# A chain of attention and feed-forward on one core: unit 0's first heads in two pieces, w_phi by two queues, unit 1's loads held, and a new order table

## The chip, the core and the metric

The kernel runs on one core of one Trainium2 chip. A core has five engines with an instruction stream each: TensorE (PE, matrix products and transposes; its weight loads are shown apart as PEld), VectorE (DVE), ScalarE (ACT), GpSimd (POOL) and SyncE (SP, which only issues DMAs). DMAs are issued from the queues of SP, ACT and POOL and move data between HBM and the on-chip memory. Engines wait for one another through semaphores; on one engine, instructions run in the order in which they were written.

The metric is the device time of one execution in microseconds (us). Beside it there is a profile of one execution, whose span runs from the first to the last instruction.

## The reference: what is computed

```python
def phi(x):                                            # x: [8, 8, 576, 64], w_phi: [64, 128]
    proj = einsum('bhsd,df->bhsf', x, w_phi)
    proj = proj - max(abs(proj), axis=-1, keepdims=True)
    return concatenate([exp(proj), exp(-proj)], axis=-1)
q_p, k_p = phi(q), phi(k)
kv  = einsum('bhsf,bhsd->bhfd', k_p, v)
z   = sum(k_p, axis=2)
num = einsum('bhsf,bhfd->bhsd', q_p, kv)
den = einsum('bhsf,bhf->bhs', q_p, z)[..., None] + 1e-06
x   = (num / den).transpose(0, 2, 1, 3).reshape(4608, 512)
h   = maximum(maximum(x @ w1, x @ w2), x @ w3)         # w1..w3: [512, 768]
out = h @ w_out                                        # w_out: [768, 512], out: [4608, 512]
```

Eight batches of eight heads go through a linear attention with a feature map of exponentials; the 4608 rows of 512 that come out go through a feed-forward layer whose activation is the greatest of three products.

## The kernel before, in words

**Units.** The 64 heads are worked off in 16 units of four heads (`attention(u)`, lines 435 to 694). A unit's heads are two pairs; a pair's 576 rows by 64 columns lie in nine tiles of 128 partitions (64 columns of each of two heads), so a unit has 18 tiles each of q, k and v. Tiles 0 to 3, 4 to 7, 9 to 12, 13 to 16 and the two tiles 8 and 17 are the groups (`GROUPS`) in which the projections are made.

**A unit's steps.** Load q, k and v. Bring q and k to bf16 (`C`, lines 450 and 475, or a load that casts, line 457). Transpose tiles on PE (`T`, lines 489 and 492) in the batches `BATCHES` of eight, eight and two tiles and copy them out of PSUM (`Tc`, line 495); from unit 4 on a DMA transposes (line 507). Project on `w2` (`G`, lines 529 and 534), take the greatest absolute values on DVE (line 553), and the exponentials of k on ACT (`Ek`, line 547). Form the exponentials of q on ACT (`Eq`, line 626) from a second product (`M`, lines 613 to 618, which uses `wphi_m` or `w2`). Weigh v by the factors `em` on POOL (`vab`, line 588). Then the products k'v (`kvps`, line 642), q'(kv) (`psn`, line 660) and the division on DVE (lines 666 and 667). The result is transposed into `xT`.

**The feed-forward layer.** Nine chunks of 512 rows: two times six `ups` products (line 713) and the products that form the output (`ops`, lines 741 and 746). It works with differences of weights: w2 - w1 and w3 - w1 are formed once (line 784), and the part that w1 contributes to the output is carried by a product w1 w_out made at the front (lines 796 and 810). The chunks are woven between later units.

**Loads at the front.** w_phi goes to two halves of the partitions by two DMAs of ACT's queue (line 359); `phi_weights` (lines 402 to 405) casts both halves into `w2` and the first once more into `wphi_m`. Unit 0's q and k come by SP in halves, a pair of heads each (line 446): q, k, k, q. Unit 1's to 3's q and k are loaded by POOL's queue, which casts on the way (line 457). The four weights of the feed-forward layer also come by POOL's queue (line 418).

**Who sets the order.** The order is written out in the table `PLAN` (lines 94 to 242): a number of a step, a letter for its engine, the buffers or PSUM banks that it takes, and the time at which a planner placed it. `plan` (line 248) reads it; the steps are then written in order of these times, so that the table fixes the order on each engine. Waits come from the data, not from the table. The planner itself isn't part of the file; the costs and delays given to each step are what it worked with. `fill` (line 266) puts fillers into PE's planned gaps while it is early: products of a constant tile that nobody reads (`idler`, line 841).

## Time and profile before

| | |
|---|---|
| three runs | 286.4, 287.06 and 288.28 us, median 287.06 |
| the profiled execution | 289.06 us, its span 287.3 us |
| mean granted TensorE clock | 0.992 |
| PE, PEld, DVE, ACT, POOL busy | 276.2, 157.3, 209.5, 192.4, 133.1 us |
| read from HBM, written to it | 34.67 MB, 9.44 MB |

How to read it: an engine's busy time is the time covered by its instructions, issues and waits not counted. A matmul's shown duration overlaps the next one's, so PE's busy share is an upper bound of its work. "idle before, releaser" says what ended an engine's idle time. A wait put down to "issue" is one for which the profile shows nothing that was waited for.

### The profile page before, as it was taken

How to read it: one execution, taken by the hardware profiler on the slowest of the kernel's cores; microseconds unless marked ns; L12 is line 12 of the kernel's file. 1: busy time of each engine (PE TensorE's matmuls, PEld its weight loads, DVE VectorE, ACT ScalarE, POOL GpSimd, SP SyncE). 2: the span in 40 equal slices, each digit the busy share in tenths (PEclk: the TensorE clock that was granted, in tenths of full speed). 3: DMA queues.
4: the chain of work that ended last, by engine and by line, in shares of the span. 5: the costliest groups of instructions: out<-in, count | busy, mean ns of one | idle time of the engine just before them, and what ended most of it. 6: DMA issues, size and time to landing. Idle time of an engine off the chain costs nothing.

```text
span 287.3 us, 8483 instructions
## 1 busy us (share of the span) xinstructions
PE 276.2 (96%) x3501; PEld 157.3 (55%) x3540; DVE 209.5 (73%) x441; ACT 192.4 (67%) x449; POOL 133.1 (46%) x119
## 2 busy tenths in 40 slices
PE   8989999999999799999999999999999999999994
PEld 3667675556665455556555555556544654444443
DVE  2899899988999677998599779968873462355330
ACT  3899899988889668877968969859469300130001
POOL 9359999769676045739171964600235001000000
PEclk9999999999999889999999999999999999999999
DMA  7999999999799999999998688474361014621334
GB/s 200 200 284 268 276 231 281 302 306 264 260 274 216 232 135 251 208 240 232 275 258 213 152 142 158 87 115 90 68 171 39 3 39 91 146 51 24 67 99 127
DMA packets 63728, 50.81 MB, mean 177 GB/s; under 512 B 46154, under 2 KB 50378, under 8 KB 63690
## 3 DMA queue, kind: packets, MB, share of 16 engines
q1 hardware_dynamic: 56686, 35.51, 56.0%
q0 software_dynamic: 6160, 13.76, 18.8%
q10 hardware_dynamic: 844, 1.00, 1.0%
q8 instruction: 27, 0.44, 0.6%
q14 instruction: 11, 0.09, 0.1%
HBM read 34.67 MB, written 9.44 MB: 154 GB/s over the span
## 4 chain that ended last, share of the span: by engine, by line
PE 89%; ACT 4%; DVE 3%; DMA 2%; issue 1%
PE ups L713 32%; PE ops L746 16%; PE ops L741 10%; PE psn L660 7%; PE kvps L642 6%; PE psm L613 5%; PE psq L534 5%; PE idler L841 3%; DMA qkT<-mT 2%; PE pm L810 2%; ACT Ek L547 2%; ACT Eq L626 2%; PE psq L529 1%; DVE mk L553 1%; DVE mqp L553 1%
## 5 line engine op out<-in xcount | busy, mean ns | idle before, releaser
L713 PE MATMUL ups<-xT,w_bf 128*128 128x512 bf16 x412 | 101.4, 379 | 1.0
L588 POOL TENSOR_TENSOR vab<-v_raw,em 128x1152 bf16<-128x1152 f32 (+1 forms) x36 | 68.0, 1904 | 47.8 <-ACT em L584 27.3
L626 ACT ACTIVATE Eq<-psm 128x512 bf16<-128x512 f32 (+1 forms) x160 | 81.0, 596 | 8.9 <-PE psm L613 8.6
L547 ACT ACTIVATE Ek<-psk 128x512 bf16<-128x512 f32 x128 | 73.5, 624 | 7.5 <-DVE mk L553 3.5
L713 PEld LDWEIGHTS <-w_bf 128*128 128x128 bf16 x432 | 40.3, 98 | 42.8 <-DVE x_sb L667 0.3
L746 PE MATMUL ops<-wout_bf,hT 128*128 128x512 bf16 (+1 forms) x214 | 51.9, 381 | 0.5 <-issue 0.2
L553 DVE TENSOR_REDUCE mqp<-psq 128x4 bf16<-128x512 f32 (+1 forms) x80 | 49.2, 632 | 4.2 <-PE psq L529 2.1
L719 DVE TENSOR_TENSOR hT<-hT,ups 128x512 bf16<-128x512 bf16 x54 | 36.2, 683 | 14.8 <-PE ups L713 13.3
L553 DVE TENSOR_REDUCE mk<-psk 128x4 f32<-128x512 f32 x64 | 42.9, 683 | 2.9 <-ACT Ek L547 2.0
L754 ACT COPY osb<-ops 128x512 f32<-128x512 f32 (+1 forms) x19 | 10.9, 575 | 39.5 <-PE ops L746 36.1
L746 PEld LDWEIGHTS <-hT 128*128 128x128 bf16 x222 | 21.6, 99 | 23.9 <-issue 1.6
L667 DVE TENSOR_TENSOR x_sb<-psn,rden 128x320 bf16<-128x320 f32 x64 | 31.5, 492 | 2.2
L660 PEld LDWEIGHTS <-Eq 128*128 128x128 bf16 x640 | 26.2, 98 | 11.5 <-issue 2.5
L660 PE MATMUL psn<-kv_sb,Eq 128*128 128x65 bf16 x640 | 28.3, 194 | 2.0 <-ACT Ek L547 2.0
L721 ACT ACTIVATE hT<-ups 128x512 bf16<-128x512 f32 x26 | 15.9, 622 | 19.9 <-PE ups L713 19.9
L723 DVE TENSOR_SCALAR hT<-ups 128x512 bf16<-128x512 f32 x28 | 18.9, 686 | 11.9 <-PE ups L713 11.7
L754 DVE COPY osb<-ops 128x512 f32<-128x512 f32 (+1 forms) x18 | 12.0, 674 | 20.0 <-PE ops L746 17.4
L741 PE MATMUL ops<-xT 128*128 128x512 bf16 x88 | 24.4, 384 | 0.4
L613 PE MATMUL psm<-qkT,wphi_m 128*128 128x512 bf16 (+1 forms) x70 | 22.4, 360 | 0.1
L534 PE MATMUL psq<-w,qkT 64*128 64x128 bf16 x256 | 21.4, 218 | 0.2 <-DVE qkT L495 0.2
L534 PE MATMUL psk<-w,qkT 64*128 64x128 bf16 x256 | 21.0, 217 | 0.5 <-DVE mqp L553 0.4
L642 PE MATMUL kvps<-vab,Ek 64*128 64x65 bf16 x1152 | 20.4, 190 | 0.6 <-issue 0.4
(76 smaller groups left out, 276.6 us busy)
## 6 DMA issues: line engine op xcount, KB each, us to landing
out_dram<-osb SPq DMA_DIRECT2D x65, 128.0 KB, 2.4
v_raw<-in_v_dram SPq DMA_DIRECT2D x13, 576.0 KB, 5.9
k_raw<-in_k_dram POOLq DMA_DIRECT2D x6, 576.0 KB, 5.6
q_raw<-in_q_dram POOLq DMA_DIRECT2D x6, 576.0 KB, 5.6
q_raw<-in_q_dram SPq DMA_DIRECT2D x6, 576.0 KB, 5.7
k_raw<-in_k_dram SPq DMA_DIRECT2D x6, 576.0 KB, 5.2
w_bf<-in_moe_w_dram POOLq DMA_DIRECT2D x3, 768.0 KB, 11.1
v_raw<-in_v_dram POOLq DMA_DIRECT2D x3, 576.0 KB, 12.2
```

Of the source, the lines that this page charges most:

```text
L534: nc.tensor.matmul(ps()[:, i, :], lhsT=cols[r, :], rhs=w2[r, c, :], start=True, stop=True)
L547: nc.scalar.activation(Ek[s]()[:, tiles_of(t0, n), :], of(1), EXP, scale=1.0 - 2.0 * s)
L553: nc.vector.tensor_reduce((mq, mk)[c]()[:, tiles_of(t0, n)], of(c), AXX, ALU.max, apply_absolute_value=True)
L588: (nc.vector if n_.eng == "DVE" else nc.gpsimd).tensor_tensor(vab()[:, g, t0:t1, 0:D], vb()[:, t0:t1, :], em()[:, g, t0:t1].unsqueeze(2).t ...
L613: nc.tensor.matmul(psm()[:, 0:w], lhsT=wphi_m, rhs=rhs, start=True, stop=True)
L626: nc.scalar.activation(Eqb()[s][:, cols], psm()[:, 0:w], EXP, scale=1.0 - 2.0 * s)
L642: nc.tensor.matmul(kvps[ab]()[:, t // NT, g, :], lhsT=Ek[g]()[r, t, :], rhs=vab()[r, g, t, :], start=(t + g == 0), stop=(t == UT - 1 and g ...
L660: nc.tensor.matmul(psn()[:, c, :], lhsT=Eqb()[g][:, t0:t0 + P], rhs=kv()[:, pr, ab, g, :], start=(g == 0), stop=(g == 1))
L713: nc.tensor.matmul(ups(), lhsT=w_bf[i + 1][:, ct, j * P:(j + 1) * P], rhs=tokens_of(ct), start=(ct == 0), stop=(ct == CT - 1))
L719: nc.vector.tensor_tensor(hT()[:, j, :], hT()[:, j, :], ups(), ALU.max)
L741: nc.tensor.matmul(ops_()[:, 0:width], lhsT=tile_of(ct, tt), rhs=line_w[c_i > MOVE][:, ct, cols], start=(ct == 0), stop=False)
L746: nc.tensor.matmul(ops_()[:, 0:width], lhsT=hT()[:, j, tt * P:(tt + 1) * P], rhs=wout_bf[:, j, cols], start=False, stop=(j == JT - 1))
```

## The change

- Unit 0's q and k come in three pieces each instead of two halves: tiles 0 to 3 and 4 to 8 of the first pair, and the second pair whole. Each piece has its own load on SP's queue and its own cast; the order on SP is q's first piece, k's first piece, q's second pair, k's second piece, q's second piece, k's second pair, then v of unit 0, which POOL's queue carried before.
- Unit 0's transposes go in batches of four, four, eight and two tiles instead of eight, eight and two; a projection waits for the batch of its own group.
- The second half of w_phi is loaded from POOL's queue, as its first DMA. The cast into `wphi_m` is a step of its own.
- The first load of unit 1 on POOL's queue, and so every load behind it, waits for a one-partition copy on DVE that reads k's first piece and writes into the buffer that the load fills.
- The casting loads of units 0 to 3 lose their split in halves (only unit 0 used it). Evictions of transposes may also go to ACT.
- The first fillers may be half as wide, and the last 0.3 instead of 0.2 of planned time ahead of the first transposes stay free.
- `PLAN` is a new table. Against the old one, w_out and w2 leave POOL's queue much later, w2 and w3 as two issues in a row; loads of v, q and k change places between SP's and POOL's queues; some evictions and copies change engine. In the last 3943 of PE's 7082 instructions the order is the same.

```diff
+BATCHES0 = [(0, 4), (4, 4), (9, 8), (8, 2)]
+PIECES = [(0, 0, 4), (0, 4, 9), (1, 0, 9)]
...
-HALVES = 1
+HELD = 0
...
-SLOW = 4.6
+SLOW = 6.0
...
+        wide = 4
         gap, t = n.start - free, max(free + 0.1, ready)
-        while gap > (0.35 if t < WARM else 0.5) and t < n.start - 0.2:
+        while gap > (0.35 if t < WARM else 0.5) and t < n.start - (0.2 if free else 0.3):
...
-                    todo.append((t, make(i)))
+                    wide = 4 if free or t < n.start - 0.9 else 2
+                    todo.append((t, make(i, wide)))
...
-            t += 0.26 if t > SLOW else 0.43
+            t += 0.26 if t > SLOW else 0.11 * wide
...
+    def piece_of(what, p, c0, c1):
+        return (q, k)[what][0, 2 * p:2 * p + 2].rearrange("ab (i c) d -> (ab i) c d", c=NT)[:, c0:c1, :]
...
-    for ab in range(2):
-        nc.scalar.dma_start(wphi_f[ab * D:(ab + 1) * D, :], w_phi)
+    nc.scalar.dma_start(wphi_f[0:D, :], w_phi)
+    nc.gpsimd.dma_start(wphi_f[D:P, :], w_phi)
...
-        nc.vector.tensor_copy(wphi_m[0:D, :], wphi_f[0:D, :])
+    def phi_rows(n_):
+        copy_on[n_.eng](wphi_m[0:D, :], wphi_f[0:D, :])
...
+            if what < 2 and u == 0:
+                for i, (p, c0, c1) in enumerate(PIECES):
+                    ts = slice(NT * p + c0, NT * p + c1)
+
+                    def main(what=what, ts=ts, p=p, c0=c0, c1=c1, raw=raw):
+                        queue_of["SP"].dma_start(raw()[:, ts, :], piece_of(what, p, c0, c1))
...
+                    first[what, i] = n_
...
+            elif what < 2 and by_pe:
+                if u == 1 and what == 0:
+                    src = raw_bufs(0)[1]
+                    need = [nd("gate", {"DVE": 0.1}, lambda src=src: nc.vector.tensor_copy(
+                        qk()[0:1, :, 0, 0:1], src()[0:1, 0:2, 0:1]), [first[1, HELD]], [src, qk])]
+                elif u > 1:
+                    need = []
+
+                def main(what=what):
+                    nc.gpsimd.dma_start(by_pairs(qk()[:, what, :, :]), rows_of(what, u, 0, 2))
...
-            for i, (t0, nb) in enumerate(BATCHES):
+            batches = BATCHES if u else BATCHES0
+            for i, (t0, nb) in enumerate(batches):
...
-                need = [0, 1] if nb == 2 else [i]
+                need = ([1, 2] if nb == 2 else [i]) if u == 0 else [0]
...
-            a = nd("G", {"PE": 0.22 if n == 2 else 0.236 * len(part)}, lambda mms=mms: [f() for f in mms], [tr[ti], n_phi],
+            a = nd("G", {"PE": 0.22 if n == 2 else 0.236 * len(part)}, lambda mms=mms: [f() for f in mms], [tr[ti] if u else tr[part[0]], n_phi],
```

## The prediction

> **What bounds the kernel now.** I read the page first (busy shares, 40 slices), then a table of stretches, then the instructions in order of time for the first 14 us and for the one stretch that stands out.

> ```profile
> PE 276.2 (96%) x3501; PEld 157.3 (55%) x3540; DVE 209.5 (73%) x441; ACT 192.4 (67%) x449; POOL 133.1 (46%) x119
> PE   8989999999999799999999999999999999999994
> PEclk9999999999999889999999999999999999999999
> ```

> TensorE (PE) is busy for 96% of the span, so a change pays only where PE isn't doing useful work: at the front, and in the one slice with a 7 (the fourteenth, from 93 us), behind which the granted clock has two 8s. The stretches say what stands beside PE at each stage. Columns: stretch, length, busy time (and instructions) of PE, PE's weight loads, DVE, ACT, POOL, granted clock, DMA share, GB/s.

> ```profile
> 0.00:8.00 8.00, 6.96 (x26) 2.81 (x27) 2.45 (x14) 3.30 (x4) 7.30 (x15) 1.00 0.78 196
> 8.00:16.00 8.00, 7.64 (x124) 5.03 (x122) 7.13 (x16) 6.92 (x15) 2.22 (x4) 1.00 1.18 211
> 16.00:24.00 8.00, 6.89 (x145) 5.17 (x144) 8.00 (x17) 7.86 (x25) 5.79 (x7) 1.00 1.15 272
> 24.00:32.00 8.00, 7.51 (x200) 5.25 (x193) 7.13 (x18) 7.04 (x19) 7.96 (x9) 1.00 1.13 283
> 32.00:40.00 8.00, 7.89 (x156) 5.98 (x159) 7.36 (x19) 7.26 (x18) 8.00 (x6) 1.00 1.12 266
> 40.00:60.00 20.00, 19.68 (x292) 11.06 (x293) 18.29 (x36) 19.47 (x47) 17.87 (x12) 1.00 1.05 269
> 60.00:94.00 34.00, 33.54 (x499) 20.46 (x505) 30.89 (x69) 29.78 (x72) 24.26 (x21) 1.00 1.04 267
> 94.00:102.00 8.00, 5.99 (x106) 3.30 (x100) 4.00 (x9) 4.24 (x11) 0.00 (x0) 0.79 1.29 210
> ```

> So: loads until 8; DVE and ACT (8.00 and 7.86 of 8 us) at 16 to 24; PE from 24 to 94, where its idle time is 0.49 + 0.11 + 0.32 + 0.46 = 1.38 us; a loss of 2 us and of clock at 94 to 102.

> The front, in order of time (start, duration, engine, line, operation; q behind an engine is its queue's issue):

> ```profile
> 0.72 1.25 ACTq L359 DMA_DIRECT2D wphi_f<-in_w_phi_dram  x2
> 0.72 0.40 SPq L446 DMA_DIRECT2D q_raw<-in_q_dram  x1
> 1.04 5.83 PE L841 MATMUL idler<-idle 128*128 128x512 bf16 x14 [1.04 <-DVE idle L411]
> 1.18 0.89 SPq L446 DMA_DIRECT2D k_raw<-in_k_dram  x2
> 1.89 0.93 POOL L457 DMA_DIRECT2D qk_bf<-in_k_dram  x1
> 2.12 0.61 SPq L446 DMA_DIRECT2D q_raw<-in_q_dram  x1
> 2.81 0.74 POOL L457 DMA_DIRECT2D qk_bf<-in_q_dram  x1
> 3.43 0.67 ACT L450 CAST qk_bf<-q_raw 128x576 bf16<-128x576 f32 x1
> 3.75 0.22 DVE L404 CAST w<-wphi_f 64x128 bf16<-64x128 f32 x1 [1.76 <-DMA wphi_f<-in_w_phi_dram]
> 5.00 0.67 ACT L450 CAST qk_bf<-k_raw 128x576 bf16<-128x576 f32 x1 [0.90 <-DMA k_raw<-in_k_dram]
> 5.83 0.22 DVE L404 CAST w<-wphi_f 64x128 bf16<-64x128 f32 x1 [1.86 <-DMA wphi_f<-in_w_phi_dram]
> 6.81 0.61 PE L489 MATMUL tps<-ident,qk_bf 128*128 128x128 bf16 x8
> 7.45 0.69 DVE L495 COPY qkT<-tps 128x1024 bf16<-128x1024 bf16 x1 [0.95 <-PE tps L489]
> 8.43 0.23 PE L534 MATMUL psq<-w,qkT 64*128 64x128 bf16 x1
> 8.68 0.67 ACT L450 CAST qk_bf<-q_raw 128x576 bf16<-128x576 f32 x1 [1.02 <-DMA q_raw<-in_q_dram]
> 8.86 1.29 DVE L553 TENSOR_REDUCE mqp<-psq 128x4 bf16<-128x512 f32 x2 [0.71 <-PE psq L534]
> 9.26 2.05 ACT L547 ACTIVATE Ek<-psk 128x512 bf16<-128x512 f32 x4
> 10.06 0.28 DVE L495 COPY qkT<-tps 128x256 bf16<-128x256 bf16 x1
> 11.14 0.73 POOL L471 DMA_DIRECT2D q_raw<-in_q_dram  x1 [0.72 <-DMA qk_bf<-in_q_dram]
> 11.84 1.24 PE L492 MATMUL tps<-ident,qk_bf 128*64 128x128 bf16 x32
> ```

> The reader is to see a chain: k's half lands at 5.00, is cast, is transposed at 6.81 (PE still worked off fillers until 6.87), evicted by 8.14, and the first projection starts at 8.43. Unit 1's transposes follow at 11.84, once its q has landed shortly before 11.14.

> **The change part by part.** In the built programs PE has 7082 rows before and after, and from row 3139 (a psm of unit 8, about 105 us) on they are the same; DVE and ACT agree from the same time on, POOL and SP some 10 and 20 us later. No PE operation goes; 26 fillers stay 26, three at half width. So what is gained must be gained ahead of 105 us, and the rest is shifted.

> *First heads in pieces.* k's first piece is SP's second issue, at 1.18. It has 4/9 of the half's bytes. The half of q took 0.72 to 3.43, 2.7 us; that of k 1.18 to 5.00, 3.8; and w_phi, 32 KB, 3.0. Smallness alone buys little, then: 2.7 to 3.8, and I take 2.7, the row of a half that had the queue to itself, since two small pieces now stand first: it lands at 3.9 (5.0). Cast of 256 columns of 576: 0.67 x 4/9 = 0.30, to 4.2. Four transposes, half of 0.61: 4.5. Eviction of 512 columns lies between 0.28 and 0.69: 0.42, so 4.9, and two hand-overs like that before 8.43 (0.29) add 0.6: first projection at 5.6, upper end 6.8. The fillers ahead of it fall from 14 to nine, three of them halves: (6 + 1.5) x 5.83 / 14 = 3.1 us, over at 4.2, out of the way.

> *Half of w_phi by GpSimd's queue.* Both halves now leave ACT's queue 0.6 us apart, yet the second is usable at 5.83, 2.1 us after the first. Issued first on POOL it should come like the first half, at 3.75; at worst it stays at 5.83, and since the eviction stands behind its cast on DVE, the projection would start at 5.83 + 0.22 + 0.42 + 0.3 = 6.8. I take 3.75, the nearest row of a first transfer on its queue. [...] No row here decides it, since both halves went through one queue.

> *DVE and ACT.* DVE's first reduction moves from 8.86 by the same 2.8 us. Ahead of unit 1 it gets two casts (0.30 + 0.37), a one-element copy (about 0.13) and two half evictions for a whole one (0.84 - 0.69), and gives the 0.28 eviction to ACT: +0.67. Its lead is about 2.1. ACT has four casts in front of its first exponential, the last of the sixth piece on SP, issued near 3.0. It lands at 3.0 + 3.8 = 6.8, if POOL's loads are really out of the way, or at 3.0 + 6.5 = 9.5, if it trails like the last half now (2.12 to 8.68). I take the first: exponentials from 7.5 instead of 9.26, a lead of 1.7; the other end is -0.9.

> *Unit 1's loads held.* POOL's first load waits for a DVE copy that stands behind the first eviction and a cast: about 6.0 instead of 1.89, the second 6.9. Queued behind them on POOL are every other load of that queue: w1, unit 2's q and k, w_out.

> ```profile
> k_raw<-in_k_dram POOLq DMA_DIRECT2D x6, 576.0 KB, 5.6
> w_bf<-in_moe_w_dram POOLq DMA_DIRECT2D x3, 768.0 KB, 11.1
> 29.79 6.29 POOL L784 TENSOR_TENSOR w_bf<-w_bf 128x1024 bf16<-128x1024 bf16 x3
> 40.72 1.46 PE L713 MATMUL ups<-xT,w_bf 128*128 128x512 bf16 x5
> 28.97 0.80 POOL L418 DMA_DIRECT2D w_bf<-in_moe_w_dram  x1
> ```

> A load of 576 KB on POOL takes 5.6 us in the run of the kernel, the held ones took up to 11.1 - 2.8 = 8.3 in the crowd. I take 5.6, the crowd being what is removed: unit 1 complete at 12.5 instead of 11.1, its transposes 0.7 later than 11.84; the other end is 15.2, 3.4 later. DVE has unit 0's reductions (nine more of 0.65) to fill until then, and PE's order puts two psm groups of unit 0 ahead of them. v of unit 0 goes to SP and stops being late.

> *What is handed on.* At 16 to 24 DVE and ACT are full, so the smaller lead, ACT's 1.7, is what they carry; unit 1 gives back 0.7. From 24 to 94 PE has 1.38 us of idle time to win or lose in, and I let the lead through. **Sum: 1.7 - 0.7 = 1.0 us**, ends 1.7 and -0.7.

> *Late fetches.* w2 and w3 now leave as two issues in a row near 29 us, the last w leaving at 28.97 today; five differences of 2.1 (6.29 / 3) follow in one run on POOL. I cost this at nothing: the first `ups` is at 40.72, and the differences are needed one by one. If that cover goes, see the third rival.

> **Against the profiled execution.** It took 289.06 us with a span of 287.3: 1.76 lies around the span and stays. 289.06 - 1.0 = 288.06. That execution lies 2.0 above the median of 287.06; I take the same 1.0 off the median: **286.1**.

> **The hole at 95 us.** It is the largest loss, and I leave it in.

> ```profile
> 95.25 0.50 PE L613 MATMUL psm<-qkT,wphi_m 128*128 128x256 bf16 x2
> 97.70 0.47 PE L660 MATMUL psn<-kv_sb,Eq 128*128 128x65 bf16 x10 [1.95 <-ACT Ek L547]
> 97.70 0.35 PEld L660 LDWEIGHTS <-Eq 128*128 128x128 bf16 x9 [2.24 <-issue]
> 98.50:102.00 3.50, 3.50 (x13) 0.51 1.36 270
> ```

> PE stands 1.95 us inside ten matmuls, and then has half the clock for 3.5 us: 1.95 + 0.49 x 3.5 = 3.7 us. The view names an ACT result, yet PE's weight loads stand for 2.24 us with nothing to wait for ("issue"), so I read it as a hold-up in getting instructions to PE, not as work that came late. In the changed order the same `psn` group stands at the same place, row 3010 of 7082, behind the same burst of 72 `kvps`. So I expect it again.

> **The rivals.**
> 1. *The gain is eaten* (0.18). The small pieces land at 5.0, or the last one trails to 9.5, or w_phi comes late, while unit 1 is 0.7 later all the same. For it: 32 KB took 3.0 us. Against it: POOL's loads are out of the way. Time 287.06 + 0 to 0.7: 287.4.
> 2. *The hole goes* (0.15). What comes before it in the queues differs (one load of unit 9 from SP where two stood), so the hold-up may not meet PE's burst. In full: 286.1 - 3.7 = 282.4 (0.08). Half: PE stands still, but the clock stays: 286.1 - 1.7 = 284.4 (0.07). [...]
> 3. *Slower: the late weights hold the MLP* (0.12). The first of the two last w loads, issued at 29 and taking the 11.1 us of its row, lands at 40.1. Its first difference ends 2.1 later, at 42.2, and PE waits 1.5 us at the first `ups`, with a clock dip of 1.7 like the one above: 287.06 - 1.0 + 1.5 + 1.7 = 289.3. It decides from a landing later than 40.72 - 2.1 = 38.6. For it: that load has no slack by the medians. Against it: two of the three w loads in that median stood in the crowd of the front.

> **How the numbers follow.** Forecast 0.55 (286.1, own range 285.4 to 287.8), rivals 0.18, 0.15, 0.12. The range 284.3 to 289.3 leaves out the hole gone in full (0.08) and what lies beyond rival 3 (some 0.08). About 1% is what a measurement of this kernel can tell from no change: 284.2 to 289.9. Faster than that 0.11 (the hole gone, and a little of the forecast), slower 0.07 (half of rival 3), within 0.82.

> **What would show it.** Right: first projection near 5.6, first exponential near 7.5, unit 1's transposes near 12.5, the first `ups` about 1 us before 40.72, the same psm of unit 8 about 1 us earlier, a gap of about 2 us in `psn` near 95. Wrong: casts of the first pieces not before 5; DVE idle behind w_phi; PE idle before unit 1's transposes; `ups` waiting for `w_bf`; slice fourteen without its 7. The forecast fails most easily by the hole: it is nearly four times the sum.

## The result, and the profile after

The changed kernel took 295.27 us (median of four, 293.37 to 295.85), the kernel before beside it 287.56: the ratio is 1.026 with an interval from 1.020 to 1.032, slower by 7.7 us. I had forecast 286.1 with a range up to 289.3. On a second chip it took 294.88 beside 287.52. Medians here are taken over all executions of a kernel, ratios over those that lie within 1.5% of its fastest, so the two can differ. The profiled execution took 295.11 us with a span of 293.3, 6.0 more than the span before.

The page: busy time, PE in 40 slices of 7.3 us, and the granted clock.

```profile
PE 277.7 (95%) x3540; PEld 157.1 (54%) x3540; DVE 212.5 (72%) x446; ACT 191.5 (65%) x445; POOL 136.0 (46%) x125
PE   8777999999999699999699999999999999999994
PEclk9999899999999999999999999999999999999999
```

Where the kernel before had a single 7, there are now three of them at 7 to 29 us, and a 6 at 95 and at 139 us. The stretches (columns as in the prediction):

```profile
0.00:8.00 8.00, 6.29 (x39) 2.65 (x39) 4.42 (x20) 2.72 (x4) 3.00 (x10) 1.00 0.71 213
8.00:16.00 8.00, 6.15 (x99) 3.97 (x100) 6.07 (x13) 7.32 (x19) 2.52 (x5) 1.00 1.11 187
16.00:24.00 8.00, 6.67 (x113) 4.84 (x115) 8.00 (x15) 7.37 (x18) 7.97 (x10) 1.00 1.00 187
24.00:32.00 8.00, 6.35 (x145) 4.75 (x142) 4.93 (x12) 5.42 (x16) 6.95 (x10) 0.79 1.14 273
94.00:102.00 8.00, 5.64 (x127) 3.65 (x126) 5.32 (x13) 5.54 (x11) 4.86 (x4) 1.00 1.19 222
120.00:200.00 80.00, 77.57 (x1086) 44.30 (x1082) 64.90 (x137) 61.55 (x148) 42.14 (x34) 1.00 0.89 195
```

PE does 6.15 us of work at 8 to 16 where it did 7.64, and 6.35 at 24 to 32 where it did 7.51, and the half clock that stood at 98 us now stands in this last stretch (0.79). At 94 to 102 it again lacks more than 2 us, now at full clock. From 120 to 200 it stands still for 2.43 us, where it had 0.68.

The front in order of time:

```profile
4.30 0.23 DVE L414 CAST w<-wphi_f 64x128 bf16<-64x128 f32 x1 [0.89 <-DMA wphi_f<-in_w_phi_dram]
5.26 0.23 PE L558 MATMUL psq<-w,qkT 64*128 64x128 bf16 x1
6.42 0.74 POOL L479 DMA_DIRECT2D qk_bf<-in_q_dram  x1 [3.88 <-DVE qk_bf L473]
8.53 0.67 ACT L465 CAST qk_bf<-k_raw 128x576 bf16<-128x576 f32 x1 [1.54 <-DMA k_raw<-in_k_dram]
9.10 2.05 ACT L571 ACTIVATE Ek<-psk 128x512 bf16<-128x512 f32 x4
13.62 1.20 PE L514 MATMUL tps<-ident,qk_bf 128*64 128x128 bf16 x36
19.50 0.87 POOL L432 DMA_DIRECT2D wout_bf<-in_moe_w_out_dram  x1
```

The first projection starts at 5.26 instead of 8.43. But the first exponential comes at 9.10, only 0.16 sooner than before, and unit 1's transposes at 13.62, 1.8 later. What PE waited for, in the whole span (us in total, times, longest), and the instructions at which it stood still:

```profile
PE psm L637 <- DMA qkT<-mT: 4.8, 2, 2.4
PE tps L511 <- ACT qk_bf L465: 1.7, 2, 1.5
PE psk L558 <- issue: 1.6, 1, 1.6
PE psk L558 <- DVE mqp L577: 1.1, 1, 1.1
```

```profile
28.23 0.11 PEld L558 LDWEIGHTS <-qkT 64*128 64x128 bf16 x3 [1.82 <-issue]
98.65 0.39 PE L637 MATMUL psm<-qkT,wphi_m 128*128 128x512 bf16 x1 [2.36 <-DMA qkT<-mT]
141.79 0.48 PE L637 MATMUL psm<-qkT,wphi_m 128*128 128x256 bf16 x2 [2.43 <-DMA qkT<-mT]
```

Three stops, then, beside the smaller waits of the front: one inside unit 2's first projection at 26.4, in which PE waits for nothing that the profile shows ("issue"), and two for `qkT<-mT`, the small DMA that writes a unit's row of maxima beside its transposed q.

To see how the loss adds up I take the same step in both kernels and subtract the time at which its own table planned it. This lag of PE, in us (from the traces and the tables; the new table ends 0.8 us earlier than the old one):

```
                          before   changed   difference
unit 0's kvps              -0.7      2.8        3.5
first ups                   0.6      6.0        5.4
unit 4's kvps               1.1      6.7        5.6
unit 6's third psm          1.1      9.2        8.1
unit 9's first psm          4.8     12.0        7.1
last product                4.9     11.7        6.8
```

6.8 - 0.8 = 6.0, the difference of the spans. So 3.5 are lost by 25 us (1.75 in time, 25.07 against 23.32; the rest is that the new table planned this step 1.7 earlier); 1.9 more up to the first `ups`, where the changed kernel loses 3.2 with the stop at 26 and its half clock, the kernel before 1.3; 2.5 at 96. The kernel before then loses 3.7 in its own hole, the changed one 2.7 at 139.

### The profile page after: what moved, and what is told of

Read it like the earlier page. It is cut to its first block, busy times and chain, and to the rows that moved or that the text cites. A ratio compares the mean times of both kernels' runs of the same rounds, so it can differ in the third digit from the quotient of the medians.

```text
span 293.3 us, 8525 instructions
## 1 busy us (share of the span) xinstructions
PE 277.7 (95%) x3540; PEld 157.1 (54%) x3540; DVE 212.5 (72%) x446; ACT 191.5 (65%) x445; POOL 136.0 (46%) x125
## 4 chain that ended last, share of the span: by engine, by line
PE 80%; DMA 7%; ACT 4%; SPq 4%; DVE 3%; issue 1%; DVEq 0%
PE ups L737 31%; PE ops L770 14%; PE ops L765 9%; PE kvps L666 6%; PE psn L684 6%; DMA qkT<-mT 5%; PE psm L637 5%; PE psq L558 4%; SPq L531 2%; ACT Ek L571 2%; DMA k_raw<-in_k_dram 2%; PE pm L834 2%; DVE mqp L577 1%; PE psq L553 1%; DVE mk L577 1%
## 5 line engine op out<-in xcount | busy, mean ns | idle before, releaser
L737 PE MATMUL ups<-xT,w_bf 128*128 128x512 bf16 x432 | 102.6, 379 | 0.0
L747 DVE TENSOR_SCALAR hT<-ups 128x512 bf16<-128x512 f32 x30 | 20.4, 685 | 11.9 <-PE ups L737 11.7
L684 PE MATMUL psn<-kv_sb,Eq 128*128 128x65 bf16 x640 | 28.9, 195 | 0.0
L745 ACT ACTIVATE hT<-ups 128x512 bf16<-128x512 f32 x24 | 14.4, 617 | 19.2 <-PE ups L737 19.0
L558 PEld LDWEIGHTS <-qkT 64*128 64x128 bf16 x512 | 14.8, 94 | 14.7 <-issue 10.8
## 6 DMA issues: line engine op xcount, KB each, us to landing
v_raw<-in_v_dram SPq DMA_DIRECT2D x8, 576.0 KB
v_raw<-in_v_dram POOLq DMA_DIRECT2D x8, 576.0 KB, 5.9
q_raw<-in_q_dram SPq DMA_DIRECT2D x8, 576.0 KB, 4.3
k_raw<-in_k_dram SPq DMA_DIRECT2D x7, 576.0 KB
k_raw<-in_k_dram POOLq DMA_DIRECT2D x5, 576.0 KB, 6.6
w_bf<-in_moe_w_dram POOLq DMA_DIRECT2D x3, 768.0 KB, 9.7
q_raw<-in_q_dram POOLq DMA_DIRECT2D x4, 576.0 KB, 6.9
```

The lines of the kernel that those rows point to most:

```text
L558: nc.tensor.matmul(ps()[:, i, :], lhsT=cols[r, :], rhs=w2[r, c, :], start=True, stop=True)
L684: nc.tensor.matmul(psn()[:, c, :], lhsT=Eqb()[g][:, t0:t0 + P], rhs=kv()[:, pr, ab, g, :], start=(g == 0), stop=(g == 1))
L737: nc.tensor.matmul(ups(), lhsT=w_bf[i + 1][:, ct, j * P:(j + 1) * P], rhs=tokens_of(ct), start=(ct == 0), stop=(ct == CT - 1))
```

## The experiments

### The changed kernel once more

> The changed kernel unaltered, on the same chip and beside the same runs of the kernel before as the three kernels below, since its runs so far and those of the first experiments lay on different chips. Theory: 295 within 1 us, the mean granted clock 0.988 to 0.994 in nearly all executions (one or two windows of 3.4 us at half clock each), the stop inside unit 2's first projection near 26 us in the profile again. Rival (bad luck in the first four executions): 291 to 293 and a clock of 1.0 in half of them.

Measured: 294.88 us (four executions, 290.54 to 296.87), ratio 1.017 (1.008 to 1.027), clocks 0.988 to 0.994 in all four. The stop is at the same instruction, 2.3 us. It was not bad luck in the sense of the rival, though one of the four took 290.54. Here no half clock followed it; it followed the wait at 94 us instead.

### The stop in the front: 84 rows more on PE

A row is one instruction of PE's program, a weight load or a matmul (a few only wait). The first 16 fillers are cut into products of a quarter of the width:

```diff
     def product(i, wide):
+        made.append(i)
+        cuts = wide if len(made) <= 16 else 1
...
+            for c in range(cuts):
-            nc.tensor.matmul(idler[:, 0:wide * P], lhsT=idle, rhs=idle.unsqueeze(1).to_broadcast([P, wide, P]),
+                nc.tensor.matmul(idler[:, c * w * P:(c + 1) * w * P], lhsT=idle,
+                                 rhs=idle.unsqueeze(1).to_broadcast([P, w, P]), start=True, stop=True)
```

> The changed kernel, with its first 16 fillers written as several products of a quarter of the width: the same PE time, 42 matmuls with their weight loads more, so that everything behind them stands 84 rows later in PE's program. Theory (instruction transfers): the changed kernel's stop of 1.8 us inside unit 2's first projection at 26.4 us, and the 3.4 us of half clock behind it, come from a block of 256 PE instructions that was asked for only at 25.85, in the middle of the 72 kvps, and arrived too late; moved by 84 rows, the border of the block lies ahead of the kvps burst, the stop goes, and with it the half clock: 3.0 to 3.5 us less, near 291.8. A new stop may then appear where another border falls right behind a kvps burst (near 180 us). Rival (late data): the projection waits for a PSUM bank or for DVE; then the stop stays at the same instruction and the time within 1 us of 295.3.

Measured: 290.28 us (median of eight, 288.27 to 295.06), ratio to the kernel before 1.010 (1.007 to 1.014): 5.0 less than the changed kernel (4.7 less, if each is taken against the kernel before beside it). The profiled execution was the longest of the eight (it lost some 4 us at 68 us to a row of maxima and a half clock behind it), so only its front is read here, PE in order of time and two of its waits:

```profile
25.32 1.27 PE L666 MATMUL kvps<-vab,Ek 64*128 64x65 bf16 x72
26.43 0.22 PE L558 MATMUL psq<-w,qkT 64*128 64x128 bf16 x1
26.85 0.28 PE L639 MATMUL psm<-qkT,w 128*128 128x256 bf16 x1
```

```profile
PE pm L834 <- DMA wout_bf<-in_moe_w_out_dram: 1.3, 1, 1.3
PE tps L514 <- DMA qk_bf<-in_k_dram: 1.0, 1, 1.0
```

The eight products of the projection run through and `psm` follows 0.42 us after the first of them: the stop is gone, without a change to any data or wait. In seven of the eight executions the granted clock was 0.997 or more. Part of the gain is taken back at once: at 28.3 PE waits for w_out, a wait that the stop had hidden. No stop came near 180 us. The gain is larger than the 3.0 to 3.5 that the stop and its half clock account for. In this one profile, SP's order being as it was, the waits for the rows of maxima of units 6 and 9 are smaller too, 0.89 us at 101 and none for unit 9, against 2.36 and 2.43; whether that is the rest of the gain isn't shown.

### The same in the kernel before

The first 14 fillers in quarters, also 84 rows.

> The kernel before, with its first 14 fillers written as four products of a quarter of the width each: again 84 rows more ahead of everything else, and the same PE time. Theory (instruction transfers): the stop of 2 us in psn at 95.6 us and the half clock behind it go, 3.0 to 3.8 us less than the kernel before, near 284. Rival (loads and transposes at 88 to 97 us hold something that PE waits for): the stop stays, and the time stays within 0.5 us of 287.5.

Measured: 286.19 us (median of ten), ratio 0.997 (0.994 to 0.999). The profiled execution has no stop at 95 us and a clock of 1.0; its longest wait behind the front is

```profile
PE psm L613 <- DMA qkT<-mT: 0.9, 1, 0.9
```

The stop went as expected, the gain was a third of what I expected. In 42 of 44 other executions of the kernel before the mean clock was 0.997 or more: the 3.5 us of half clock in its profiled execution (0.992) are not what it usually pays.

### 114 rows: a border where I want it

> The kernel before with 19 of its 26 fillers in quarters: 114 rows more on PE instead of 84. The two borders seen lay at rows 706 and 3010, that is 194 behind a multiple of 256. Shifted by 114 rows, the border at row 2754 falls on the first instructions of unit 6's projection right behind unit 4's kvps, where the kernel before and the shift of 84 have none. Theory (instruction transfers): a stop of 1 to 2.5 us appears there, near 83 us, with a request for instructions inside that kvps burst, and perhaps a shorter one inside unit 6's kvps near 94; 0.5 to 3 us slower than the shift of 84 rows (286.2). Rival (the stops belong to what is done at 26 us and at 95 us, not to rows): no stop at 83 us, and the time within 0.5 us of 286.2.

Measured: 286.07 us (median of ten), ratio 0.996 (0.994 to 0.999), and no stop at the place named:

```profile
82.69 1.26 PE L642 MATMUL kvps<-vab,Ek 64*128 64x65 bf16 x72
83.78 0.22 PE L534 MATMUL psq<-w,qkT 64*128 64x128 bf16 x1
```

So a border behind a burst isn't enough. The DMA records of the trace tell the difference: the request for this block was sent at 77.72, 6 us ahead of the projection.

### 24 rows: does the stop follow the row?

The first four fillers in quarters.

> The changed kernel with only its first 4 fillers in quarters: 12 weight loads and matmuls more, 24 rows. In all six kernels with the rows of the changed kernel PE stood still right behind its 350th weight load, at 25 to 30 us, whatever the front had done before. Theory (instruction transfers, border at a row): the stop stays behind the 350th weight load, which is now one of the last four pairs of unit 0's kvps and no longer the sixth pair of unit 2's projection; 1 to 2.5 us long, the time within 1.5 us of 295. Rival (the projection waits for something): the stop stays in front of the same psk, which is now behind the 362nd weight load. Third: no stop, if the request comes earlier because the border lies inside the burst.

Measured: 294.7 us (292.29 to 297.6). PE in order of time:

```profile
24.11 1.17 PE L666 MATMUL kvps<-vab,Ek 64*128 64x65 bf16 x65
27.32 0.29 PE L666 MATMUL kvps<-vab,Ek 64*128 64x65 bf16 x7 [2.04 <-issue]
```

The stop moved out of the projection into the kvps in front of it, and stands again behind the 350th weight load. The rival is dead: nothing that the projection waits for can stop the kvps. The records of PE's instruction transfers (16 KB each) in ten of the fourteen profiles, against its 350th weight load, behind which this border lies:

```
                    request   350th load   next load   request to next
changed               25.85        26.31       28.23        2.38
changed, again        25.36        25.20       27.79        2.43
SP order              25.29        25.46       27.57        2.28
v on POOL's queue     25.46        26.98       28.09        2.63
not held              30.35        30.22       32.69        2.34
w_phi by ACT          25.87        26.32       28.25        2.38
24 rows               25.07        25.07       27.32        2.25
before                23.56        25.64       25.64
84 rows, changed      22.69        25.82       25.82
84 rows, before       21.22        25.24       25.25
```

Where the request goes out less than 2 us ahead of the 350th load, PE stands still until 2.25 to 2.63 us after the request, though the transfer itself takes 0.9 to 1.1. Where it goes out 2.1 us ahead or more, there is no stop. The border at 95 us in the kernel before lies nine blocks of 256 rows behind this one: its request went out at 94.33, 1.0 us ahead, the transfer took 2.04, and PE went on at 97.70, 3.4 us behind the request.

The same can be counted at every border of all fourteen profiles, 371 of them, with the rows of the built programs. At eleven the request went out less than 2 us ahead, and at each of these the weight loads stood still, for 0.4 to 2.5 us: the seven above, the one at 95 us, and three more between 31 and 41 us that cost 0.4 to 0.5. At the 360 others, with 2.08 us or more, the longest pauses were 0.24, 0.26 and 0.42 us, the last two with the request 8 to 9 us ahead. That a block has 256 rows the traces show by count: in the kernel before the requests at 23.56 and 94.33, for the borders behind rows 706 and 3010, lie nine transfers and 2304 rows apart; its profile and the one after have 27 transfers each for PE's 7082 rows. Why one request leaves 6 us ahead and another in the last moment isn't shown. Waiting for data ahead of the border does not tell them apart: in the 6 us ahead of the stop PE idled for 0.3 us at most in the seven profiles that have it here, in the kernel before, which has none here, for 1.1. What differs is that the burst of 72 `kvps` began 1.2 us ahead of this border in the changed kernel (25.07 and 26.31), 2.3 us ahead in the kernel before (23.32 and 25.64); but with 114 rows a border behind such a burst cost nothing.

### The order on SP

Two places in the table: x of unit 5 (438) behind unit 6's row of maxima (472, at 85.5), and two loads behind unit 9's row (667, at 124.4).

```diff
-438S@84.1 ... 1025S0@121.6 765S1@122.0
+438S@85.6 ... 1025S0@124.5 765S1@124.6
```

SP's queue of the changed kernel, then of the kernel before, at the first place:

```profile
82.38 0.81 SPq L593 DMA_DIRECT2D qkT<-mT  x1
90.86 1.36 SPq L714 DMA_TRANSPOSE xT<-x_sb  x1
92.32 0.78 SPq L593 DMA_DIRECT2D qkT<-mT  x1
93.44 3.40 SPq L531 DMA_TRANSPOSE qkT<-qk_bf  x1
```

```profile
82.03 1.73 SPq L690 DMA_TRANSPOSE xT<-x_sb  x1
86.73 0.80 SPq L569 DMA_DIRECT2D qkT<-mT  x1
```

Before, a transpose of x was issued 4.7 us ahead of the row of maxima, now 1.5 us ahead.

> The changed kernel with another order on SP at two places: the transpose of unit 5's x is issued behind unit 6's row of maxima (qkT<-mT) instead of 1.5 us ahead of it, and the two loads of q and k ahead of unit 9's row of maxima go behind it. Theory (queue order): unit 6's row then lands some 3 us earlier than 98.6 and the wait of psm of 2.4 us at 96 goes; unit 9's row is issued 1.9 us earlier, and the wait of 2.4 us at 139 shrinks to 0.5 or less: 4 to 4.9 us less than the changed kernel, near 290.8. Rival (crowd): unit 6's row is slow because the five POOL loads issued from 81 to 88 us fill the DMA engines until 94; then the first wait stays at 2 us or more and only the second shrinks, near 293.2.

Measured: 291.54 us (four executions, 288.75 to 293.05), ratio 1.014 (1.007 to 1.020), 3.7 less than the changed kernel (3.4 less, each against the kernel before beside it). PE's longest waits:

```profile
PE psk L558 <- issue: 1.8, 1, 1.8
PE psm L637 <- DMA qkT<-mT: 1.3, 1, 1.3
PE ups L737 <- DMA xT<-x_sb: 1.1, 1, 1.1
PE kvps L666 <- POOL vab L612: 0.9, 1, 0.9
```

Both waits for the row of maxima at 96 and 139 us are gone, the first by the exchange of two issues, with POOL's five loads as they were: the crowd is not the reason. They are gone in all three profiles with this order, and at least one of them is there in all eight with the old one, from 0.9 to 4.8 us in total, so the order on the queue is what makes PE wait at these places, and how long it waits depends on more than that. The 1.3 us that are left stand at 106 us, for the row of unit 8, which is issued 1.7 us behind a transpose of x, as unit 6's was. At the second place something else is late now: unit 9's kvps wait for POOL, and a chunk's `ups` for a transpose of x that stands further back on SP.

### Both together

> The changed kernel with both the fillers in quarters (84 more rows ahead on PE) and the new order on SP at two places. If the two causes are independent their gains add: 295.3 - 5.0 - 3.7 = 286.6, level with the kernel before within 0.5 us. If the stop in the front hides behind it waits that the SP order removes too (rival: same loss counted twice), it stays at 289.5 to 290.5. What is left above the kernel before is then the front: PE's lag at unit 0's kvps and at the first pm (waiting for w_out, landed 29.3).

Measured: 292.76 us (290.61, 290.72, 294.8 and 296.45), ratio 1.019 (1.009 to 1.029). The gains don't add: its two best lie where the shift of rows alone lay. The profiled execution (290.72) has neither the stop nor a wait for the row of maxima worth naming. Its waits:

```profile
PE ups L737 <- DMA xT<-x_sb: 1.4, 1, 1.4
PE kvps L666 <- POOL vab L612: 1.3, 1, 1.3
PE pm L834 <- DVE x_sb L691: 1.1, 1, 1.1
```

The last line names DVE, but the product starts at 28.18 and w_out landed at 28.13, so I put this wait down to w_out. POOL, in front of unit 9's kvps:

```profile
130.28 1.14 POOL L496 CAST qk_bf<-q_raw 128x1152 bf16<-128x1152 f32 x1 [6.85 <-DMA q_raw<-in_q_dram]
131.90 4.19 POOL L612 TENSOR_TENSOR vab<-v_raw,em 128x1152 bf16<-128x1152 f32 x2
```

POOL stands 6.85 us at the cast of a q that has not landed, with the products for unit 9 queued behind it. In the changed kernel this was there too (6.59 us), under the wait for the row. This execution's lag is 1.8 at unit 0's kvps, 3.2 at the first `ups`, 4.2 at unit 9's first psm and 7.2 at the end; the 84-row kernel before has 0.1, 0.8, 2.2 and 2.8. 7.2 - 0.8 - 2.8 = 3.6, the difference of their profiled times (290.72 and 286.91) but 0.2. Why two of the four executions took 294.8 and 296.45 isn't shown; neither was profiled.

### The front: unit 1's loads not held

```diff
-                    need = [nd("gate", {"DVE": 0.1}, lambda src=src: nc.vector.tensor_copy(
-                        qk()[0:1, :, 0, 0:1], src()[0:1, 0:2, 0:1]), [first[1, HELD]], [src, qk])]
+                    need = [nd("gate", {"DVE": 0.1}, lambda: None, [first[1, HELD]], [src, qk])]
```

> The changed kernel without the copy on DVE that holds unit 1's first load; POOL's queue starts with w_phi and goes on at once. Theory (the hold costs): unit 1's loads send their first packets near 5.4 us instead of 7.5, all loads behind them (w1, unit 2, w_out, unit 3, w2, w3) land 1.5 to 2 us earlier, w_out near 27.5; PE's lag at unit 0's kvps falls by 0.5 to 1.5 us and the time by 0.5 to 2. Rival (the hold pays): without it k's second pair lands 1 us later than 8.5, the first exponential at 10 instead of 9.1, and the time rises by 0.5 to 1.5.

Measured: 296.64 us (295.3 to 299.55), ratio 1.034 (1.027 to 1.041).

```profile
10.46 0.67 ACT L465 CAST qk_bf<-k_raw 128x576 bf16<-128x576 f32 x1 [3.09 <-DMA k_raw<-in_k_dram]
11.04 1.08 ACT L570 ACTIVATE Ek<-psk 128x512 bf16<-128x512 f32 x2
18.15 1.20 PE L513 MATMUL tps<-ident,qk_bf 128*64 128x128 bf16 x36
```

The rival has it: without the hold the last piece comes 1.9 us later, and unit 1's q and k land at 10.9 and 13.6, little different from with it (11.4 and 13.0). Unit 1's transposes, the last line, come at 18.15 instead of 13.62. The hold pays for itself in this front.

### The front: w_phi back on ACT's queue

> The changed kernel with both halves of w_phi on ACT's queue, as before. By the forecast's lower value POOL's queue made the second half usable at 3.75; the changed kernel shows 4.28. If the queue matters (theory), the second half is usable near 5.8 as in the kernel before, and the first projection starts near 6.5 instead of 5.26. [...]

Measured: 291.99 us, one execution, from which no change of time can be told. DVE's two casts of w_phi:

```profile
3.32 0.22 DVE L414 CAST w<-wphi_f 64x128 bf16<-64x128 f32 x1 [0.15 <-DMA wphi_f<-in_w_phi_dram]
4.65 0.22 DVE L414 CAST w<-wphi_f 64x128 bf16<-64x128 f32 x1 [1.11 <-DMA wphi_f<-in_w_phi_dram]
```

The second half is usable at 4.65, against 4.30 and 4.84 in the two profiles of the changed kernel, and the first projection starts at 5.64 (5.26 and 5.64). The queue makes no difference that shows in this one execution. The same queue had given 5.83 in the kernel before, so what brought w_phi forward is something that runs beside it; which, isn't shown.

### The front: v of unit 0 elsewhere

v behind unit 1's loads on POOL's queue (`19S0@3.5` becomes `19G0@7.2`):

> The changed kernel with v of unit 0 on POOL's queue, behind unit 1's two held loads, instead of last on SP's. Theory (v crowds the pieces): k's second pair lands near 7.0 instead of 8.5, its cast and the transposes of the second pair come 1.3 to 1.5 us earlier, the first exponential at about 7.7 instead of 9.1, and PE's lag behind the old kernel at unit 0's kvps (1.8 us) halves; the time falls by 0.7 to 1.5 us, unless the stop at 26 us grows. Rival 1 (rate): the six pieces are limited by the rate of their own transfers, k's second pair still lands at 8 or later and nothing changes. Rival 2 (unit 1 decides): the pieces come earlier, but unit 1's transposes stay at 13.6 and the time within 0.5 us.

Measured: 293.2 us (four executions, 289.0 to 295.75), ratio 1.012 (1.004 to 1.020). The executions spread too widely to tell a gain. ACT in order of time, and a wait of PE:

```profile
6.95 0.67 ACT L465 CAST qk_bf<-k_raw 128x576 bf16<-128x576 f32 x1
7.82 2.07 ACT L571 ACTIVATE Ek<-psk 128x512 bf16<-128x512 f32 x4 [0.20 <-PE psk L558]
PE pwT L820 <- DMA w_bf<-in_moe_w_dram: 1.8, 1, 1.8
```

Without v behind them the pieces come early: the cast stands at 6.95 and the exponentials at 7.82, near the 7.5 of the prediction. That v is what delays them is only in part shown. In the eight other profiles that hold unit 1's loads and have v on SP, this cast starts at 7.26, 7.39, 7.43, 7.54, 7.69, 8.53, 8.54 and 8.78, so v costs between next to nothing and 1.8 us, and two executions of the same changed kernel differ by 1.3 us (8.53 and 7.26). But v now stands in front of w1, w1 lands 2.5 us later (19.55 against 17.08), PE waits 1.8 us for it, and unit 0's kvps come later than in the changed kernel (25.81 against 25.07). Next, v behind w1 (`19G0@8.0`), with the shift of 84 rows:

> The changed kernel with 16 fillers in quarters (the shift of 84 rows) and v of unit 0 on POOL's queue behind w1 instead of last on SP's. With v between unit 1's loads and w1, the cast of k's second pair came at 6.95 instead of 8.53, but w1 landed at 19.55 instead of 17.1 and PE waited 1.9 us for it. Theory (each load that is moved pushes the next): the cast comes at 7, w1 lands at 16.5 to 17.5, and now v is late: it lands near 18.3, POOL's first products of unit 0 start 1.5 to 2 us later than 16.4 and unit 0's kvps stay at 24 us or later; the time 289 to 291, as with the shift alone (290.3). Rival (v was the one load too many in the front): kvps of unit 0 come at 23 or earlier and the time falls to 288.5 or below.

Measured: 295.09 us (four executions, 291.78 to 298.45), ratio 1.031 (1.024 to 1.038). In the profiled execution (291.78) the cast starts at 7.38, no earlier than in several with v on SP; unit 0's kvps start at 24.28 and stop twice inside for POOL's products, since v landed at 19.05; w_out, issued behind those products, lands at 29.94:

```profile
PE pm L834 <- DMA wout_bf<-in_moe_w_out_dram: 1.5, 1, 1.5
PE kvps L666 <- POOL vab L612: 1.0, 2, 0.6
```

That each moved load pushes the next is as expected; the time is 4 us worse than I said, and why isn't shown.

### w_out one place earlier

With the shift and the new SP order, w_out ahead of unit 1's v (`1092G@17.8` becomes `1092G@15.8`).

> As the kernel with fillers in quarters and the new SP order, and w_out's load on POOL's queue one place earlier, ahead of unit 1's v. Theory (late w_out): w_out lands near 25.8 instead of 27.4, the wait of PE ahead of the first pm (1.1 to 1.25 us at 27 us in the two kernels without the stop) goes, and what follows is 1 us earlier; v of unit 1 lands 3.7 us later, near 26, and its first use on POOL stands at 26.9, so it isn't late by more than 0.5. In time 0.5 to 1.2 us less than that kernel's undisturbed 290.6. Rival: unit 1's v is late instead, POOL's products and the second kvps come 1 us later, and the time stays.

Measured: 293.7 us (291.96 to 295.36), ratio 1.021 (1.012 to 1.030). w_out landed at 25.84 and the wait for it is gone, but other waits took its place:

```profile
PE ups L737 <- POOL w_bf L808: 2.2, 2, 1.2
PE psk L558 <- DVE mqp L577: 1.8, 1, 1.8
```

The first is the third rival of the prediction: v of unit 1 is late (27.51), POOL's products for it push the differences of the weights, and the `ups` wait. The second stands at 20 us, in front of the first use of w_out; unit 1's q and k had landed late (13.29 and 14.73), before w_out was issued at 16.41, so it isn't shown to come from this edit. That this order could be put right by moving one load isn't supported by any of the three tries.

## Why the prediction was wrong, point by point

Two steps failed. The front, priced at 1.0 us of gain, lost 0.6 to 1.8 us by unit 0's `kvps`. And the step that lets everything from 24 us on through unchanged, with only the old hole in it, put at nothing what the new order itself makes PE wait for: a stop of 1.6 us with 1.7 us lost to half clock behind it at 26 us (3.41 us at 0.50, from 28.38), and two waits of 2.4 us for rows of maxima. As an estimate from the two profiled executions: 1.8 + 1.6 + 1.7 + 4.8 make 9.9; less the 3.7 of the old hole, which did not come, that is 6.2, and the spans differ by 6.0.

- **First projection at 5.6.** Measured 5.26 and 5.64. Right. w_phi was usable at 4.30 and 4.84, later than my 3.75, which I had taken for a first transfer on a queue of its own; with both halves on ACT's queue it was usable at 4.65, in one execution.
- **DVE and ACT, a lead of 1.7.** Wrong for ACT, whose lead was the term of the sum; DVE's first reduction did come 2.8 us sooner, at 6.03. I took the last piece at 6.8, "if POOL's loads are really out of the way". They were, and in the first profile it was cast at 8.53 and the first exponential started at 9.10, a lead of 0.16; in the second at 7.26 and 8.22, a lead of 1.0. v of unit 0 stands behind this piece on the same queue. My text has v go to SP "and stops being late", at no price; against the two profiles without v there (6.95 and 7.38) its price is anything from nothing to 1.6 us. What moves this cast by 1.3 us between two executions of the same kernel isn't shown.
- **Unit 1 held, +0.7.** Measured +1.8 (13.62 against 11.84). In the second profile the first transpose starts at 12.51, as forecast, and the others wait for k until 13.58. I had unit 1 complete at 12.5; its k landed at 13.03 and 13.54. The size was off. And the hold is not what costs: without it, in this front, these transposes come at 18.15.
- **What is handed on, 1.7 - 0.7.** Neither term stood. Unit 0's kvps came 1.8 us later than before in the first profile (25.07 against 23.32), 0.6 later in the second (23.96).
- **Late fetches at nothing.** I priced w2 and w3, and they did not hold PE in the changed kernel. w_out, which the same sentence of the change names, I did not price at all: it lands at 29.33 instead of 24.29, and holds PE for 1.1 to 1.5 us in three kernels without the stop (84 rows, 84 rows with the SP order, v behind w1), hidden under the stop in the changed kernel itself.
- **From 24 to 94 and behind 105 us only shifted.** Wrong; the two waits are 4.8 us of the profiled execution, and the other order on SP took 3.7 off the time. That PE's order is the same behind row 3139 says nothing of what it waits for. SP's order differed until 20 us behind that; I had noted it and given it no price. Two waits of 2.4 us for a DMA of 4.5 KB followed.
- **The hole at 95 us.** The reading was right, a hold-up in getting instructions, and wrong in its use. I expected it at row 3010 again; it came at row 706, another border of the same kind, because the request for that block went out 0.5 us ahead of it, where it had been 2.1 us. At row 3010 the request went out 5.9 us ahead, and nothing stood. And in the kernel before the half clock is rare, and the shift that takes the hole away gained 1 us of the median (287.25 against 286.19), not 3.7.
- **The rivals.** None held the time. The second's condition came true, the hole went in full, and the time rose all the same, since what replaced it was larger. The third has the right kind of mechanism (weights late for the MLP), and showed in one experiment only.

Of the 7.7 us, then, 5.0 go with the shift of rows and 3.7 with the order on SP, each alone; together they give no more than the first alone. In the one profile of both together waits for POOL, for a transpose of x and for w_out, 1.1 to 1.4 us each, come up behind them; and the shift alone had, in its one profile, already left only 0.9 us of the waits that the SP order is to remove. With either, 3 us and more above the kernel before remain. They lie with the new order of loads as a whole; moving single loads, three times, did not win them back, and which part of the order costs them stays open.

## What to carry to other kernels

A stop without a releaser ("issue") that stands behind the same ordinal number of instruction, whatever happens before it, was here an instruction border. Move such a border with a few cheap instructions (here the same fillers in narrower pieces) before reading anything into the order around it. Of a re-planned order, price what each queue is given to do, SP's small DMAs and each load by name, and not only the compute engines; an unchanged order on one engine promises no unchanged waits. When a wait is taken away, look at what was finished only just under its cover.
